# Chunked attention and a low-rank mixer: the last twelve tiles in three groups of four instead of four groups of three

## The chip, the cores and the metric

The kernel runs on one core of one Trainium2 chip. The metric is the device time of one execution in microseconds (us), the median of several runs. The engines are PE (matrix products; its weight loads are listed apart as PEld), DVE (vector work), ACT (activations), POOL (GpSimd) and SP (SyncE, which here only issues transfers).

## The reference

```python
# q, k, v: (8 batches, 8 heads, 576 positions, 64), fp32
q_c = q.reshape(B, H, nc, 64, D)            # 9 chunks of 64 positions; the same for k and v
scores = scale * np.matmul(q_c, k_c.transpose(0, 1, 2, 4, 3))
scores = scores - np.max(scores, axis=-1, keepdims=True)
attn = np.exp(scores)
attn = attn / (np.sum(attn, axis=-1, keepdims=True) + 1e-09)
x = np.matmul(attn, v_c)                    # heads side by side: x is (8, 576, 512)
u = x + (x.transpose(0, 2, 1) @ U @ V).transpose(0, 2, 1)     # U 576 x 32, V 32 x 576
out = u + np.maximum(u @ w_ch1, 0.0) @ w_ch2                  # 512 -> 2048 -> 512
```

## The kernel before

The 8 x 576 positions are 36 tiles of 128 positions, four pairs of batches with nine tiles each; tile T is number t = T mod 9 of pair T div 9, and names in the program end in pair and tile (`av0_3_1` is tile 28). All large products are made from fp32r values split into a high and a low part, three products for one (high x high, high x low, low x high).

A tile's attention takes these steps. q and k were laid out again in HBM by transfers (`halvings`), are loaded (`load`), and turned on DVE in 32 x 32 squares (`qT`, `kT`, L463). `scores` makes `sc` on PE: 32 small matmuls of 64 x 64. DVE takes the maxima (`mx`) and subtracts them (`ex`), ACT makes the exponentials, and SP's queue writes them to HBM and fetches them back re-laid (`es`), so that one more DVE transpose gives `eT`. `values` makes `av` on PE, 32 small matmuls again; DVE divides by the sums and leaves `x`. For the mixer, PE makes `y` (from `x` and U, `project_ops`) once a batch's tiles are there, and `u` (from `y` and V, L692); DVE adds `u` to `x` (L698); `x` then goes through HBM and a DVE transpose (`us`, `uT`), or for the first pair through four PE transposes (`ut`, L704), and is split by ACT (`uth`, L724) and DVE (`utl`, L729).

The channel product runs over groups of three tiles, 384 columns. For each of 16 blocks f of 128 hidden channels, `hidden` makes twelve matmuls (`h`, L757), `relu_high` on ACT (L766) and `relu_low` on DVE (L771) leave `hh` and `hl`, and one block later `project_out` (L784), called by `flush` tile by tile, adds three 512-column matmuls per tile into that tile's accumulator (`o`, one PSUM bank per tile, eight banks in all). After the last block `finish` (L796) adds the residual `x` and SP's queue writes the tile out.

Groups 0 and 1 are ordered by a planner that knows costs. From group 2 on, the work on later tiles is put between the flushes by lists of words, spread evenly over a group's slots: `n` load, `t` turn q and k, `s` scores, `q` turn the exponentials, `a` the last step (`av` and its division), `p` one step of `y`, `l`, `f`, `u` the three steps of the mixer, `h` a halving transfer. `scores` brings the previous tile's last step with it:

```python
        soft = behind[-1][0]
        done = behind.pop(0)[2] if len(behind) > 1 else []
        return [*done, *soft]
```

A scheduler then settles the order of instructions within each engine, near to where the program's order has them. Residuals `x` stay in SBUF (nine buffers) from their attention to their `finish`.

Of the kernel before, what the change touches and what calls it, by code (L numbers as in the profile page):

```python
# [22 lines left out]
def kernel(  # L23
# [17 lines left out]
    P = 128  # L41
# [44 lines left out]
    ident = const.tile([P, P], F32, name="ident")  # L86
    make_identity(nc, ident)
    warm = const.tile([P, 1], F32, name="warm")
    nc.scalar.activation(warm, ident[:, 0:1], AF.Exp)
# [52 lines left out]
    def begin_filling():  # L142
        spare["a"] = const.tile([P, 512], mybir.dt.bfloat16, name="fill")
        nc.vector.memset(spare["a"], 0.0)
        spare["ps"] = bank("ps_fill")
        fill(7)
# [232 lines left out]
    ut_of = {}  # L379
# [23 lines left out]
    def load_qk(pr, t):  # L403
# [63 lines left out]
    def attention_ops(pr, t, *after):  # L467
# [48 lines left out]
        def maximum(e):  # L516
            if e == 0:
                st["ex"] = slot(tag_e, F32, "ex_" + n, (P, HP, 2, C) if own else (P, 2, C // SQ, HP, SQ))
                st["mx"] = work.tile([P, 2, HP], F32, tag="mx", name="mx_" + n, bufs=2)
# [44 lines left out]
        def sums():  # L564
            sm = st["sm"] = work.tile([P, 2, HP], F32, tag="sm", name="sm_" + n, bufs=2)
# [66 lines left out]
    def project_ops(pr, e, xs):  # L632
        steps = []
        prev = None
        for i in range(5):
# [3 lines left out]
            def high(i=i, n=n, st=st):  # L639
                st["h"] = slot("uT", F32R, "xh_" + n)  # L640
                nc.scalar.copy(st["h"], x_of[pr, i + 4 * e])  # L641
# [28 lines left out]
            steps.append([h, lo, prev])  # L670
# [11 lines left out]
    def mix_ops(pr, t, x, ys, after=None, first=None):  # L682
        n = f"{pr}_{t}"
        st = {}
        g, j = divmod(t, GT)
# [19 lines left out]

        def put_u():
            st["kept"] = put(x_of[pr, t], "us_" + n, by_channel=True)

        def fetch_u():
            st["us"] = fetch(st["kept"], slot("us", F32, "us_" + n, (P, P // SQ, P)))  # L710

        def square_u():
            uT = st["t"] = slot("uT", F32, "uT_" + n)
# [4 lines left out]
        def high():  # L718
            if j == 0:
                ut_of[pr, g] = [  # L720
                    work.tile([P, NCC, GN], F32R, tag="ut" + z, name=f"ut{z}_{pr}_{g}", bufs=2) for z in "hl"
                ]
            ptv = st["t"].rearrange("p (c t) -> p c t", c=NCC)
            nc.scalar.copy(ut_of[pr, g][0][:, :, j * P : (j + 1) * P], ptv)  # L724

        def low():
            uh, ul = ut_of[pr, g]
            js = slice(j * P, (j + 1) * P)
            nc.vector.tensor_sub(ul[:, :, js], st["t"].rearrange("p (c t) -> p c t", c=NCC), uh[:, :, js])  # L729
# [4 lines left out]
        if (pr, t) == (0, 0):  # L734
            Op("PE", 0.01, end_filling, lr, free="bank")
        if pr > 0:
# [5 lines left out]
            return [[lr, ad, pu], [fe], [tr, hi, lo]]  # L742
# [6 lines left out]
    def hidden(pr, g, f):  # L749
        uh, ul = ut_of[pr, g]  # L750
        ps = bank(f"h_{pr}_{g}_{f}")
        w = w1[f]
        prods = [(0, uh), (0, ul), (1, uh)]
        n = 0
        for cc in range(NCC):
            for z, u in prods:
                o = nc.tensor.matmul(  # L757
                    ps[:, :GN], lhsT=w[:, z, cc], rhs=u[:, cc, :], start=(n == 0), stop=(n == 3 * NCC - 1)
                )
                n += 1  # L760
# [32 lines left out]
    def finish(pr, g, f, j, ps):  # L793
        t = g * GT + j
        x = x_of[pr, t]
        nc.vector.tensor_add(x, ps, x)  # L796
        if f == NF - 1:
            r0 = pr * 2 * S + t * P
            nc.sync.dma_start(out_f[r0 : r0 + P], x)

    def block_ops(pr, g, f, first, final, after, prev):
# [3 lines left out]
        def h():  # L805
            st["ps"] = hidden(pr, g, f)

        def rh():
            st["hh"] = relu_high(pr, g, f, st["ps"])

        def rl():
            st["hl"] = relu_low(pr, g, f, st["ps"], st["hh"])

        def out(j):
            st[j] = project_out(pr, g, f, (st["hh"], st["hl"]), first, final, j)
# [7 lines left out]
        for j in range(GT):  # L823
            d = Op("PE", 0.7, lambda j=j: out(j), c, d, take="bank" if first else "", free="h" if j == GT - 1 else "")
            if final:
                ends.append(
                    Op("DVE", 0.69, lambda j=j: finish(pr, g, f, j, st[j]), d, free="bank x" if last else "bank", lat=2.0)
# [13 lines left out]
    TAIL = 6  # L841
# [9 lines left out]
    for item in WORK:  # L851
# [13 lines left out]
        else:  # L865
            for t in range(GT * i, GT * i + GT):
# [14 lines left out]
    for g, f0, f1 in STRETCHES:  # L881
        for f in range(f0, f1):
            rank[0] = BASE
            prev = block_ops(0, g, f, f == 0, f == NF - 1, [*w_done[f], *mixed[g]], prev)
# [36 lines left out]
    tiles = [(pr, t) for pr in range(NPAIR) for t in range(NT)]  # L921
    pend = None

    def flush(j):
        if pend is not None:
            pr, g, f, hs = pend
            ps = project_out(pr, g, f, hs, f == 0, f == NF - 1, j)
            if f == NF - 1:
                finish(pr, g, f, j, ps)
# [3 lines left out]
    def attend(pr, t, what):  # L933
# [16 lines left out]
    LATER = {  # L950
# [95 lines left out]
```

## Time and profile before

| | us |
|---|---|
| median of 3 runs (lowest to highest) | 940.14 (939.91 to 940.99) |
| the profiled execution: its time | 939.42 |
| its span in the trace | 937.6 |
| granted clock of PE, mean | 0.996 |

The profile is that of one execution. Spans, starts and waits are microseconds of its span, which is 1.8 us shorter than the execution's time. PE's matmuls overlap, and their ends are modelled, so that a matmul's cost is read from the start of one to the start of the next. A granted clock of 1.00 is the upper of PE's two levels, 2.4 GHz.

### The profile page before, as it was taken

How to read it: one execution, taken by the hardware profiler on the slowest of the kernel's cores; microseconds unless marked ns; L12 is line 12 of the kernel's file. 1: busy time of each engine (PE TensorE's matmuls, PEld its weight loads, DVE VectorE, ACT ScalarE, POOL GpSimd, SP SyncE). 2: the span in 40 equal slices, each digit the busy share in tenths (PEclk: the TensorE clock that was granted, in tenths of full speed). 3: DMA queues.
4: the chain of work that ended last, by engine and by line, in shares of the span. 5: the costliest groups of instructions: out<-in, count | busy, mean ns of one | idle time of the engine just before them, and what ended most of it. 6: DMA issues, size and time to landing. Idle time of an engine off the chain costs nothing.

```text
span 937.6 us, 16153 instructions
## 1 busy us (share of the span) xinstructions
PE 916.5 (98%) x6639; PEld 806.1 (86%) x6642; DVE 488.7 (52%) x922; ACT 212.3 (23%) x379; POOL 30.1 (3%) x84
## 2 busy tenths in 40 slices
PE   7789999999999999999999999999999999999998
PEld 4569999878898888888898898988889889999997
DVE  6789999975545535553434534553433643321211
ACT  5434343322211212121211221111121211111110
POOL 5510000000000000000000000000000000000000
PEclk9999999999999999999999999999999999999999
DMA  9980688546646535563543733562231512310000
GB/s 214 222 260 1 140 168 185 138 129 146 143 98 150 127 57 130 124 127 81 129 92 79 153 70 79 150 140 68 78 91 35 148 45 46 79 23 1 35 1 34
DMA packets 271449, 98.79 MB, mean 105 GB/s; under 512 B 221296, under 2 KB 257136, under 8 KB 271376
## 3 DMA queue, kind: packets, MB, share of 16 engines
q1 hardware_dynamic: 269440, 94.81, 44.5%
q0 software_dynamic: 1328, 2.80, 1.4%
q8 instruction: 52, 0.85, 0.4%
q10 hardware_dynamic: 608, 0.15, 0.1%
q14 instruction: 21, 0.17, 0.1%
HBM read 73.84 MB, written 37.75 MB: 119 GB/s over the span
## 4 chain that ended last, share of the span: by engine, by line
PE 91%; DMA 3%; DVE 3%; issue 1%; ACT 1%; SPq 0%; POOL 0%; DVEq 0%; ACTq 0%
PE h L757 43%; PE o L784 41%; DMA qkv<-in_q_dram 2%; PE av L555 2%; PE sc L507 2%; PE u L692 1%; PE y L652 1%; PE y L653 1%; DMA vall<-vroom 1%; PE y L659 1%; PE ps_fill L151 0%; DVE eT L463 0%; PE ps_qT L477 0%; DMA us<-us_3d 0%; PE ps_kT L477 0%
## 5 line engine op out<-in xcount | busy, mean ns | idle before, releaser
L757 PE MATMUL h<-uth,w 128*128 128x384 f32 x1536 | 413.5, 337 | 1.6 <-DVE ex L528 1.6
L784 PE MATMUL o<-w,hh 128*128 128x512 f32 x1152 | 346.6, 393 | 0.0
L757 PEld LDWEIGHTS h<-uth,w 128*128 128x128 f32 x1536 | 279.8, 188 | 10.6 <-issue 1.4
L757 PE MATMUL h<-utl,w 128*128 128x384 f32 x768 | 258.1, 336 | 1.3 <-DVE utl L729 1.3
L784 PEld LDWEIGHTS o<-w,hh 128*128 128x128 f32 x1152 | 213.8, 188 | 36.7
L784 PE MATMUL o<-w,hl 128*128 128x512 f32 x576 | 214.2, 396 | 0.0
L771 DVE SCALAR_TENSOR_TENSOR hl<-h,hh 128x384 fp32r<-128x384 f32 x192 | 105.5, 549 | 203.3 <-ACT hh L766 202.8
L766 ACT ACTIVATE hh<-h 128x384 fp32r<-128x384 f32 x192 | 94.4, 491 | 458.7 <-PE h L757 458.5
L757 PEld LDWEIGHTS h<-utl,w 128*128 128x128 f32 x768 | 144.1, 188 | 7.9 <-DVE utl L729 1.6
L784 PEld LDWEIGHTS o<-w,hl 128*128 128x128 f32 x576 | 107.4, 188 | 22.9
L463 DVE STREAM_TRANSPOSE uT<-us 128x512 f32<-128x512 f32 x27 | 29.6, 1097 | 50.7 <-PE h L757 26.9
L463 DVE STREAM_TRANSPOSE eT<-es 128x512 f32<-128x512 f32 x27 | 29.1, 1079 | 41.0 <-DMA es<-es_6d 9.5
L463 DVE STREAM_TRANSPOSE qT<-qn 128x512 f32<-128x512 f32 x27 | 19.1, 709 | 46.4 <-PE h L757 44.7
L536 ACT ACTIVATE ex<-ex 128x512 f32<-128x512 f32 x36 | 22.8, 634 | 72.4 <-DVE ex L528 60.2
L641 ACT CAST xh<-x 128x512 fp32r<-128x512 f32 x30 | 18.5, 618 | 69.7 <-DVE x L574 44.7
L698 DVE TENSOR_TENSOR x<-u,x 128x512 f32<-128x512 f32 x36 | 24.2, 685 | 19.2 <-PE u L692 19.0
L521 DVE TENSOR_REDUCE mx<-sc 128x4 f32<-128x256 f32 x72 | 27.9, 413 | 5.4 <-PE sc L507 5.4
L724 ACT CAST uth<-uT 128x512 fp32r<-128x512 f32 x27 | 16.7, 620 | 53.6 <-DVE uT L463 53.6
L574 DVE TENSOR_TENSOR x<-av,sm 128x256 f32<-128x256 f32 x72 | 27.2, 419 | 1.4 <-DMA out_dram<-x 0.3
L414 POOL MEMSET vn<- 128x8 f32 x27 | 3.1, 114 | 689.1 <-PE av L555 506.3
L796 DVE TENSOR_TENSOR x<-o,x 128x512 f32<-128x512 f32 x36 | 23.1, 677 | 3.6 <-PE o L784 3.6
L645 DVE TENSOR_TENSOR xl<-x,xh 128x512 fp32r<-128x512 f32 x30 | 20.6, 686 | 7.6 <-ACT xh L641 6.8
(85 smaller groups left out, 531.7 us busy)
## 6 DMA issues: line engine op xcount, KB each, us to landing
wraw<-in_moe_w_ch_dram SPq DMA_DIRECT2D x32, 512.0 KB
out_dram<-x SPq DMA_DIRECT2D x36, 256.0 KB
halfq<-in_q_dram SPq DMA_DIRECT2D x24, 288.0 KB
halfk<-in_k_dram SPq DMA_DIRECT2D x24, 288.0 KB
qn<-halfq SPq DMA_DIRECT2D x27, 256.0 KB
kn<-halfk SPq DMA_DIRECT2D x27, 256.0 KB
vn<-in_v_dram SPq DMA_DIRECT2D x108, 64.0 KB
qkv<-in_v_dram POOLq DMA_DIRECT2D x36, 64.0 KB, 7.3
```

Of the source, the lines that this page charges most:

```text
L463: turned = nc.vector.transpose(dst, src)
L507: nc.tensor.matmul(ps[e][cs, hp * C : (hp + 1) * C], lhsT=st["qT_"][rows, hp, cs], rhs=st["kT_"][rows, hp, cs], start=True, stop=True,)
L521: nc.vector.reduce_max(mx, st["sc"][e], axis=AX.X)
L536: nc.scalar.activation(exf, exf, AF.Exp, scale=SCALE)
L574: nc.vector.tensor_mul(by_head[:, heads(pr, t, e), :], st["av"][e][:, :, 0:D], st["sm"][:, e].unsqueeze(2).broadcast_to([P, HP, D]),)
L645: nc.vector.tensor_sub(st["l"], x_of[pr, i + 4 * e], st["h"])
L698: nc.vector.tensor_add(x, st["u"], x)
L757: o = nc.tensor.matmul(ps[:, :GN], lhsT=w[:, z, cc], rhs=u[:, cc, :], start=(n == 0), stop=(n == 3 * NCC - 1))
L766: nc.scalar.activation(hh, ps[:, :GN], AF.Relu)
L771: nc.vector.scalar_tensor_tensor(hl, ps[:, :GN], 0.0, hh, op0=ALU.max, op1=ALU.subtract)
L784: nc.tensor.matmul(acc[g, j], lhsT=h[:, js], rhs=w2[f][:, z], start=(first and i == 0), stop=(final and i == 2),)
L796: nc.vector.tensor_add(x, ps, x)
```

## The change

Tiles 0 to 23 stay in eight groups of three. Tiles 24 to 35 become three groups of four: 24 to 27, then 30, 31, 28, 29, then 32 to 35; their `hidden` matmuls have 512 columns, with 48 blocks in place of 64. What goes with it:

- The words now carry the slot at which they are due, one list for each group from 2 on. `scores` no longer brings the previous tile's last step; that is the word `a`. The product of a `y` step is a word of its own (`y`).
- The split transposed input `ut` becomes one constant pair of buffers of six tiles, in which a group has its place (`PLACES`); `hh`, `hl`, the identity and the filler share one constant `hbuf`; the softmax sums live in a column of `vn`, and `mx` has one buffer.
- The residuals of tiles 21 to 35 are written to HBM (`put_rest`) and read back (word `r`) on GpSimd's queue. q, k and v of tiles 29 to 35 are loaded on that queue too.
- Tile 27 is transposed on PE (`TURNED`), not through HBM and DVE.
- Tiles 27, 30, 31, 34 and 35 (`LATE`) get their high and low split behind the last `hidden` of the group before; at the end of those groups the pending `project_out` is done at once.

```diff
+    WIDE = 24
+    KEPT = 21
+    GROUPS = [[T, T + 1, T + 2] for T in range(0, WIDE, 3)]
+    GROUPS += [[24, 25, 26, 27], [30, 31, 28, 29], [32, 33, 34, 35]]
+    PLACES = [0, 3, 0, 3, 0, 3, 0, 3, 0, 2, 0]
+    LATE = {7: [27], 8: [30, 31], 9: [34, 35]}
+    TURNED = (27,)
...
+    hbuf = const.tile([P, 4, 512], F32R, name="hbuf")
...
+    ident = hbuf[:, 3, 3 * P :].bitcast(F32)
...
+    ut = [const.tile([P, NCC, 6 * P], F32R, name="ut" + z) for z in "hl"]
...
-                nc.sync.dma_start(
+                queue = nc.sync if pr * NT + t < 29 else nc.gpsimd
+                queue.dma_start(
...
-                queue = nc.gpsimd if early(pr, t) else nc.sync
+                queue = nc.gpsimd if early(pr, t) or pr * NT + t >= 29 else nc.sync
...
-            steps.append([h, lo, prev])
+            steps.append([h, lo])
+            steps.append([prev])
...
+        def put_rest():
+            if T >= KEPT:
+                rest[pr, t] = dram.tile([P, DM], F32, name="rest_" + n)
+                nc.gpsimd.dma_start(rest[pr, t], x_of[pr, t])
+
...
+        if T in TURNED:
+            tr = Op("PE", 0.55, transposed, ad, take="bank")
+            hi = Op("ACT", 0.59, high, tr)
+            lo = Op("DVE", 0.69, low, hi, free="bank")
+            return [[lr, ad, put_rest], [], [tr], [hi, lo]]
...
-            return [[lr, ad, pu], [fe], [tr, hi, lo]]
+            return [[lr, ad, pu], [fe, put_rest], [tr], [hi, lo]]
...
-        soft = behind[-1][0]
-        done = behind.pop(0)[2] if len(behind) > 1 else []
-        return [*done, *soft]
+        return behind[-1][0]
...
-        1: "l6 t0 f6 s0 l7 n1 u6 f7 h t1 q0 s1 l8 n2 u7 f8 h t2 q1 s2 h n3 h u8 t3 . q2 s3 h n4 . .",
...
+        "h@0 t29@1 l24@2 q28@3 m30@3 a28@5 f24@6 s29@7 l25@8 u24@11 w24@11 f25@12 t30@13 l26@14 q29@15 m31@15 a29@17 u25@18 w25@18 f26@18 s30@18 u26@23 w26@23 t31@25 q30@27 p@27 m32@28 a30@29 s31@30 y@31 p@31 y@33 p@34 y@36 p@37 q31@38 y@39 a31@40 p@43 y@46 t32@49 l27@51 m33@51 s32@53 r21@54 u27@55 r22@56 r23@58",
...
+        elif kind == "r":
+            x_of[at] = work.tile([P, DM], F32, tag="x", name=f"rest_{T}", bufs=NX)
+            nc.gpsimd.dma_start(x_of[at], rest[at])
...
+    for g, words in enumerate(LISTS, 2):
...
+        late = [z for T in LATE.get(g, []) for z in (f"u{T}", f"w{T}") if z not in asked]
+        width = len(GROUPS[g])
...
+            for j in range(width + 1):
+                while words and int(words[0].split("@")[1]) <= slots:
+                    go(words.pop(0).split("@")[0])
                 slots += 1
...
+                if f == NF - 1 and j > 0 and late:
+                    go(late.pop(0))
+                flush(j)
+            pend = g, f, hs
+        assert not words and not late
+        if g in LATE:
+            for j in range(width):
+                flush(j)
+            pend = None
```

In the rows below a name ends in the numbers of pair and tile (`av0_3_1`: first half of the `av` of tile 28, number 1 of the last pair) or of group and tile, and in a buffer's number. On PE, around the `av` of tile 28 and the scores of tile 29, before:

```order
L784 MATMUL o_2_5_5980<-w_8_1457,hh_2_1_8_6269 128x512 x2
L555 MATMUL av0_3_1_6281<-vn_3_1_6014,eT_3_1_6273 64x65 x2
L555 MATMUL av1_3_1_6282<-vn_3_1_6014,eT_3_1_6273 64x65 x2
...
L555 MATMUL av1_3_1_6282<-vn_3_1_6014,eT_3_1_6273 64x65 x2
L507 MATMUL sc0_3_2_6306<-kT_3_2_6251,qT_3_2_6249 64x64 x2
L507 MATMUL sc1_3_2_6307<-kT_3_2_6251,qT_3_2_6249 64x64 x2
```

Before, the scores follow the `av` directly. After:

```order
L807 MATMUL o_7_0_5808<-w_0_248,hbuf_76 128x512 x3
L565 MATMUL av0_3_1_5812<-vn_3_1_5506,eT_3_1_5781 64x65 x2
L565 MATMUL av1_3_1_5813<-vn_3_1_5506,eT_3_1_5781 64x65 x2
...
L565 MATMUL av1_3_1_5813<-vn_3_1_5506,eT_3_1_5781 64x65 x2
L807 MATMUL o_7_1_5836<-w_0_248,hbuf_76 128x512 x3
L807 MATMUL o_7_2_5844<-w_0_248,hbuf_76 128x512 x3
L517 MATMUL sc0_3_2_5848<-kT_3_2_5761,qT_3_2_5759 64x64 x2
L517 MATMUL sc1_3_2_5849<-kT_3_2_5761,qT_3_2_5759 64x64 x2
```

Six `project_out` matmuls now stand between the two runs. On PE, around the `av` of tile 30 and the scores of tile 31, before:

```order
L784 MATMUL o_2_7_6679<-w_2_1072,hh_2_2_2_6700 128x512 x2
L784 MATMUL o_2_8_6683<-w_2_1072,hh_2_2_2_6700 128x512 x2
L555 MATMUL av0_3_3_6719<-vn_3_3_6364,eT_3_3_6714 64x65 x2
L555 MATMUL av1_3_3_6720<-vn_3_3_6364,eT_3_3_6714 64x65 x2
...
L555 MATMUL av1_3_3_6720<-vn_3_3_6364,eT_3_3_6714 64x65 x2
L507 MATMUL sc0_3_4_6744<-kT_3_4_6706,qT_3_4_6704 64x64 x2
```

This was one run of 64. After:

```order
L807 MATMUL o_7_2_5844<-w_6_1297,hbuf_76 128x512
L565 MATMUL av0_3_3_6140<-vn_3_3_5785,eT_3_3_6106 64x65
L807 MATMUL o_7_0_5808<-w_6_1297,hbuf_76 128x512
L565 MATMUL av0_3_3_6140<-vn_3_3_5785,eT_3_3_6106 64x65
L565 MATMUL av1_3_3_6141<-vn_3_3_5785,eT_3_3_6106 64x65 x2
...
L565 MATMUL av1_3_3_6141<-vn_3_3_5785,eT_3_3_6106 64x65 x2
L807 MATMUL o_7_1_5836<-w_6_1297,hbuf_76 128x512
L517 MATMUL sc0_3_4_6167<-kT_3_4_6098,qT_3_4_6096 64x64 x2
```

The `av` is now broken after its first matmul, and another `project_out` matmul stands between it and the scores. On DVE, around the `eT` of tile 30 (`eT_3_3`), before:

```order
L771 SCALAR_TENSOR_TENSOR hl_2_2_1_6667<-h_2_2_1_6652,hh_2_2_1_6665 128x384
L645 TENSOR_TENSOR xl_3_0_2_6675<-x_3_2_6477,xh_3_0_2_6673 128x512
L463 STREAM_TRANSPOSE qT_3_4_6704<-qn_3_4_6536 128x2x2x4x32
L463 STREAM_TRANSPOSE eT_3_3_6714<-es_3_3_6507 128x4x128
L771 SCALAR_TENSOR_TENSOR hl_2_2_2_6702<-h_2_2_2_6687,hh_2_2_2_6700 128x384
L463 STREAM_TRANSPOSE kT_3_4_6706<-kn_3_4_6537 128x2x2x4x32
```

and after, where `hbuf` written from `h` is what was `hl`:

```order
L531 TENSOR_REDUCE mx_3_3_6037<-sc0_3_3_6018 128x4
L531 TENSOR_REDUCE mx_3_3_6037<-sc1_3_3_6019 128x4
L538 TENSOR_TENSOR ex_3_3_6036<-sc0_3_3_6018,mx_3_3_6037 128x4x2x32
L538 TENSOR_TENSOR ex_3_3_6036<-sc1_3_3_6019,mx_3_3_6037 128x4x2x32
L473 STREAM_TRANSPOSE uT_2_8_6074<-us_2_8_6014 128x4x128
L795 SCALAR_TENSOR_TENSOR hbuf_76<-h_7_5_6050,hbuf_76 128x384
L745 TENSOR_TENSOR utl_86<-uT_2_8_6074,uth_85 128x4x128
L473 STREAM_TRANSPOSE qT_3_4_6096<-qn_3_4_5955 128x2x2x4x32
L473 STREAM_TRANSPOSE eT_3_3_6106<-es_3_3_6045 128x4x128
L795 SCALAR_TENSOR_TENSOR hbuf_76<-h_7_6_6078,hbuf_76 128x384
L473 STREAM_TRANSPOSE kT_3_4_6098<-kn_3_4_5956 128x2x2x4x32
```

The order `qT`, `eT`, `relu_low`, `kT` stays; ahead of it now stand the softmax pieces of the same tile (`mx`, `ex`), the `uT` transpose of tile 26 and its `low` step, with one `relu_low` among them.

## Rows read from the trace of the kernel before

**Rows 1.** The profile's first block: busy time of each engine, its share of the span, and instructions.
```profile
PE 916.5 (98%) x6639; PEld 806.1 (86%) x6642; DVE 488.7 (52%) x922; ACT 212.3 (23%) x379; POOL 30.1 (3%) x84
```

**Rows 2.** Busy time by stretch of the span; columns: the stretch in us, its length, busy us and instructions of PE, PEld, DVE, ACT and POOL, the clock granted to PE, the busy share of the DMA engines, GB/s.
```profile
600.00:700.00 100.00, 100.00 (x790) 89.21 (x789) 44.53 (x96) 18.20 (x35) 0.57 (x5) 1.00 0.40 95
...
800.00:900.00 100.00, 100.00 (x507) 90.79 (x506) 23.23 (x38) 13.70 (x27) 0.00 (x0) 1.00 0.12 32
```

**Rows 3.** The waits of PE from 215 us to 932 us: what it waited for, us in total, times, longest.
```profile
PE y L652 <- DVE x L574: 0.2, 1, 0.2
```

**Rows 4.** The chain that ended last, its final pieces: start, length, what.
```profile
898.59 2.08 PE h L757 x12
900.67 2.06 PE o L784 x9
...
923.47 2.08 PE h L757 x12
...
933.69 0.69 DVE x L796
```

**Rows 5.** Timeline of PE where an `av` run and an `sc` run stand together: start us, length us, what (the length is that from the first start to the modelled end of the last matmul, so that pieces overlap; what counts here are the starts).
```profile
664.25 1.31 PE L784 MATMUL o<-w,hh 128*128 128x512 f32 x5
665.49 0.70 PE L555 MATMUL av<-vn,eT 64*64 64x65 f32 x32
666.00 0.65 PE L507 MATMUL sc<-kT,qT 64*64 64x64 f32 x32
666.58 0.96 PE L784 MATMUL o<-w,hl 128*128 128x512 f32 x3
667.38 0.34 PE L757 MATMUL h<-uth,w 128*128 128x384 f32 x1
```

**Rows 6.** Timeline of PE where an `av` run stands alone, same columns.
```profile
550.50 0.40 PE L784 MATMUL o<-w,hh 128*128 128x512 f32 x1
550.82 0.70 PE L555 MATMUL av<-vn,eT 64*64 64x65 f32 x32
551.45 0.50 PE L784 MATMUL o<-w,hh 128*128 128x512 f32 x1
551.79 0.39 PE L784 MATMUL o<-w,hl 128*128 128x512 f32 x1
```

**Rows 7.** Timeline of PE where an `sc` run stands alone.
```profile
585.00 0.40 PE L784 MATMUL o<-w,hl 128*128 128x512 f32 x1
585.33 0.69 PE L507 MATMUL sc<-kT,qT 64*64 64x64 f32 x32
585.96 0.73 PE L784 MATMUL o<-w,hh 128*128 128x512 f32 x2
586.52 0.39 PE L784 MATMUL o<-w,hl 128*128 128x512 f32 x1
```

**Rows 8.** Timeline of PE where an `av` run is broken in two.
```profile
460.35 1.31 PE L784 MATMUL o<-w,hh 128*128 128x512 f32 x5
461.60 0.33 PE L555 MATMUL av<-vn,eT 64*64 64x65 f32 x2
461.85 0.49 PE L784 MATMUL o<-w,hl 128*128 128x512 f32 x1
...
463.36 0.50 PE L784 MATMUL o<-w,hl 128*128 128x512 f32 x1
463.69 0.39 PE L784 MATMUL o<-w,hh 128*128 128x512 f32 x1
```

**Rows 9.** Timeline of PE around one of the four-transpose turns of the first pair of batches.
```profile
197.84 0.60 PE L704 MATMUL ut<-ident,x 128*128 128x128 f32 x4
198.19 0.71 PE L784 MATMUL o<-w,hh 128*128 128x512 f32 x2
198.75 0.40 PE L784 MATMUL o<-w,hl 128*128 128x512 f32 x1
```

**Rows 10.** Timeline of DVE and of PE's weight loads around the scores of one tile; in brackets the idle time before a piece and what ended it.
```profile
725.63 1.04 DVE L463 STREAM_TRANSPOSE eT<-es 128x512 f32<-128x512 f32 x1
...
726.53 0.54 DVE L771 SCALAR_TENSOR_TENSOR hl<-h,hh 128x384 fp32r<-128x384 f32 x1
...
726.99 0.69 DVE L463 STREAM_TRANSPOSE kT<-kn 128x512 f32<-128x512 f32 x1
...
727.73 0.56 PEld L507 LDWEIGHTS sc<-kT,qT 64*64 64x64 f32 x32 [0.22 <-DVE kT L463]
```

**Rows 11.** Timeline of SyncE's queue and of DVE around the trip of one tile's softmax values through HBM, and one row of the list of what DVE stood idle for ahead of the `eT` transposes (us, times).
```profile
761.68 0.36 SPq L459 DMA_DIRECT2D es_8d<-ex  x1
...
764.02 0.33 SPq L400 DMA_DIRECT2D es<-es_8d  x1
...
764.92 0.56 DVE L771 SCALAR_TENSOR_TENSOR hl<-h,hh 128x384 fp32r<-128x384 f32 x1 [1.52 <-ACT hh L766]
...
766.83 1.09 DVE L463 STREAM_TRANSPOSE eT<-es 128x512 f32<-128x512 f32 x1 [1.35 <-DMA es<-es_8d]
...
  DMA es<-es_6d: 9.5, 3
```

**Rows 12.** The loads of the first pair of batches that GpSimd's queue issues: duration of one issue in ns as min/median/max, first and last start; and the time from issue to landing.
```profile
L438 POOL DMA_DIRECT2D qkv<-in_v_dram x36: 615/615/950, 2.6 to 50.9; - x36
...
DMA to landing us min/median/max: 4.3/7.3/8.3
```

More of the change, by code (lines that the diff above doesn't have):

```diff
@@ L378 @@
     y_of = {}
-    ut_of = {}
+    rest = {}
     halves = {}
@@ L640, in high @@
                 st["h"] = slot("uT", F32R, "xh_" + n)
-                nc.scalar.copy(st["h"], x_of[pr, i + 4 * e])
+                split = nc.scalar.copy(st["h"], x_of[pr, i + 4 * e])
+                if pr == NPAIR - 1:
+                    sync = mybir.DependencyInfo(mybir.DependencyClass.Sync, mybir.DependencyReason.DATA)
+                    tc.add_manual_dep(split.ins, hidden_last[-1].ins.name, sync, reason="not before this block")
             def low(i=i, n=n, st=st):
@@ L684, in mix_ops @@
         st = {}
-        g, j = divmod(t, GT)
+        T = pr * NT + t
+        g = next(i for i, z in enumerate(GROUPS) if T in z)
+        at = PLACES[g] + GROUPS[g].index(T)
+        j = 0 if T == min(GROUPS[g]) else 1
         def low_rank():
@@ L826, in block_ops @@
                 ends.append(
-                    Op("DVE", 0.69, lambda j=j: finish(pr, g, f, j, st[j]), d, free="bank x" if last else "bank", lat=2.0)
+                    Op("DVE", 0.69, lambda j=j: finish(g, f, j, st[j]), d, free="bank x" if last else "bank", lat=2.0)
                 )
@@ L840 @@
     GATES = (25, 27)
-    TAIL = 6
     HALVES_FROM = 8
@@ L865 @@
         else:
-            for t in range(GT * i, GT * i + GT):
+            for t in GROUPS[i]:
                 m = mix_ops(0, t, xs[t], ys, first=his.get(i))[1]
@@ L970, in go @@
             return
-        kind, i = word[0], int(word[1:])
-        if kind == "n":
-            key = pr + (g > 0) + i // NT, i % NT
-            if key[0] < NPAIR:
-                load(*key)
+        if kind in "py":
+            do(steps.pop(0))
             return
+        T = int(word[1:])
+        at = divmod(T, NT)
         if kind in "tsqa":
-            at = pr + 1 if g else pr
-            if at < NPAIR:
-                do(attend(at, i, {"t": "turn", "s": "scores", "q": "square", "a": "last"}[kind]))
-            return
@@ L998 @@
+    for g, words in enumerate(LISTS, 2):
+        words = words.split()
         slots = 0
+        asked = [z.split("@")[0] for z in words]
+        late = [z for T in LATE.get(g, []) for z in (f"u{T}", f"w{T}") if z not in asked]
+        width = len(GROUPS[g])
+        last = g == len(GROUPS) - 1
         for f in range(NF):
-            ps = hidden(pr, g, f)
-            hh = relu_high(pr, g, f, ps)
-            hs = hh, relu_low(pr, g, f, ps, hh)
-            for j in range(GT + 1):
-                slots += 1
-                while done < len(steps) and done * (NF * 4 - TAIL) < len(steps) * slots:
-                    go(pr, g, steps[done])
-                    done += 1
-                if j < GT:
-                    flush(j)
@@ L1010 @@
-            pend = (pr, g, f, hs)
-        assert done == len(steps)
+            ps = hidden(g, f)
+            hh = relu_high(g, f, ps)
+            hs = hh, relu_low(g, f, ps, hh)
+            for j in range(width + 1):
+                while words and int(words[0].split("@")[1]) <= slots:
+                    go(words.pop(0).split("@")[0])
+                slots += 1
+                if f == NF - 1 and j > 0 and late:
+                    go(late.pop(0))
+                flush(j)
+            pend = g, f, hs
@@ L1012 @@
+        assert not words and not late
[3 more added lines that the diff above has]
+            pend = None
     with tc.manual_schedule(engines=None):
-        for j in range(GT):
+        for j in range(len(GROUPS[-1])):
             flush(j)
-    assert not to_halve
+    assert not to_halve and not steps
 _INS = ["q", "k", "v", "moe_U", "moe_V", "moe_w_ch1", "moe_w_ch2"]
```

134 lines of the change are left out of this document (57 added, 77 removed), and 10 rows, old and new, of tables (LATER, LISTS).

## The prediction

> **What bounds the kernel now.** I read the busy table first: PE is busy 916.5 of 937.6 us, 98% of the span, and the next engine, DVE, 52% [rows 1]. A share over the whole span can hide stages, so the table by stretches came next: between 600 and 700 us PE is busy for all of the 100 us at a granted clock of 1.00, and the same between 800 and 900; DVE has 44.5 and 23.2 us of work there and the DMA engines 40% and 12% [rows 2]. The list of waits says the same from the other side: from 215 to 932 us PE waited for another engine once, for 0.2 us [rows 3]. So the time is that of the PE stream: a microsecond more or less of PE work is a microsecond of the end, and everything on DVE, ACT and the queues counts only where it makes PE stand. The chain that ended last gives the prices: the twelve 384-column matmuls of `hidden` take 2.08 us, the nine 512-column matmuls of `project_out` 2.06 us, and from 898.59 to 923.47 six blocks pass, (923.47 - 898.59) / 6 = 4.147 us each; after the last matmul there is one 0.69 us addition [rows 4].
>
> **The wide groups.** The last twelve tiles need 4 x 16 = 64 blocks of 12 + 9 matmuls; afterwards 3 x 16 = 48 blocks of 12 + 12, all of 512 columns. The number of columns that pass is the same (12 x 384 x 64 = 12 x 512 x 48), so only the cost per column can change. Before: 64 x 4.147 = 265.4 us. After, if a 512-column `hidden` matmul costs what a 512-column `project_out` matmul costs, 2.06 / 9 = 0.229 us (0.2294 with the digits that the six blocks give): 48 x 24 x 0.2294 = 264.3. That is -1.1 us. The other bound takes the rate of `hidden` itself, 173.5 ns for 384 columns, 231.3 for 512: 48 x 12 x (231.3 - 229.4) ns = 1.1 us back, so 0. I take -1.1, since the new matmul has the shape of `project_out`. A rule speaks here too: the Trainium skill, "TensorE: Matmul & The Clock Gate", on back-to-back issue, has a warm matmul cost its columns at 2.4 GHz plus about 2.5 ns. By the page 768 matmuls of 162.5 ns would become 576 of 215.8 ns, -0.5 us, and the sum below would be 0.6 higher; the rows are 7% above its figures at both sizes, so its offset is not used.
>
> **More separate runs of small matmuls.** The attention of a tile is two runs of 32 matmuls on 64 x 64 parts of the array, `av` and `sc`. Before, `scores` of a tile brought the previous tile's `av` with it, so that the two stand as one run. The new lists issue them by separate words, and the order of PE shows them apart, with `project_out` between. What that costs is read from starts. A pair: from 664.25 to 667.38 lie the run and eight `project_out` matmuls, 3.13 - 8 x 0.2294 = 1.29 us for the pair [rows 5]. `av` alone: 550.50 to 551.79 less two, 0.83 us [rows 6]. `sc` alone: 585.00 to 586.52 less three, 0.83 us [rows 7]. So a pair that is parted costs 0.83 + 0.83 - 1.29 = 0.37 us. A tile whose `av` is broken by one `project_out` matmul: 460.35 to 463.69 less seven, 1.73 us, 0.44 more than the whole pair [rows 8]. The rows show where it goes: the matmul ahead of a run lasts 550.82 - 550.50 = 0.32 us from its start to that of the run, not 0.229, and the one behind it 0.34 [rows 6]; the rest is the run's own beginning and end. The Trainium skill, "TensorEngine Tiling (Array Packing)", Key Properties, states that changing the tiling mode drains TensorE. It gives no figure; by it the price hangs on the number of entries and not on that of the matmuls, and a count of matmuls alone (the same before and after) would put this term at 0 and the sum at 940.
>
> Counted in the order of PE from the scores of tile 27 on, there are 11 runs before and 24 after: seven pairs are parted and six runs more come from `av` or `sc` broken in pieces. 7 x 0.37 + 6 x 0.44 = **+5.2 us**. The bounds: at least the lengthened neighbours, 0.09 + 0.11 = 0.20 us each [rows 6], 13 x 0.20 = 2.6; at most 0.44 for every one, 5.7.
>
> **Tile 27 turned on PE.** Four transposes come into the PE stream, and a trip through HBM with a DVE transpose goes. From 197.84 to 198.75 lie four transposes and two `project_out` matmuls: 0.91 - 0.46 = **+0.45 us** [rows 9].
>
> **Waits of PE on DVE.** PE's one listed wait comes with a y product; the weight load for the scores at 727.73 stood 0.22 us for `kT` as well, which stands on DVE behind `eT` and a `relu_low` [rows 10]. The same order (`qT`, `eT`, `relu_low`, `kT`) is there after, but groups 6 and 7 hold four to five attention tiles rather than three, and uT transposes with their `low` steps come close ahead. The trip of the softmax values takes 766.83 - 761.68 = 5.15 us from its first issue to the `eT` that waited for it, and another tile's `eT` waited 9.5 / 3 = 3.2 us for them three times [rows 11] without holding PE, since DVE had nothing due. In the new lists a tile's square (`q`) stands 8 to 11 slots behind its scores (`s29@7`, `q29@15`), a slot being a quarter of a 4.15 us block or a fifth of a wide one of 24 x 0.2294 = 5.5 us, so 1.0 to 1.1 us. The trip with some 3 us of softmax ahead of it (my estimate from the pieces around it) then just fits, with no slack to speak of. I take +0.3 us over before; the bounds are 0 and +3.
>
> **Costed at nothing.** The residuals of tiles 21 to 35 make 15 transfers out and 15 in of 256 KB. The DMA engines are busy 40% and later 12% of the time [rows 2], and a residual is asked for (`r` words) nine or more slots ahead of its addition, some 10 us, where loads on GpSimd's queue land in 4.3 to 8.3 us [rows 12]. Without that cover the one addition and its output wait, not PE, except at the tail, where the last `r` stands a block and more ahead. The loads of tiles 29 to 35 move from SyncE's queue to GpSimd's: an issue costs 615 ns there [rows 12], SyncE gets that time free, and GpSimd has nothing else. Wider `relu_high` and `relu_low` lie beside 5.5 us of PE per block. At the ends of groups 7, 8 and 9 the pending `project_out` is done at once behind the last `hidden`; the late uT split (ACT, DVE) and the last `relu` pair are covered by 24 of these matmuls, 2 x 2.75 us, and if they weren't, PE would stand for what is missing, three times. The tail stays: one 0.69 us addition behind the last matmul [rows 4]; each tile's three matmuls, 0.69 us, keep pace with it. The one conversion more at the start (128 columns, on DVE) is a fraction of a microsecond at most, once, and I give it nothing.
>
> **Sum.** -1.1 + 5.2 + 0.45 + 0.3 = +4.9 us on the profiled execution's 939.42, 944.3; the median of the runs is 0.72 above that execution, so **945.0 us**. With all bounds: low -1.1 + 2.6 + 0.45 + 0 = +2.0, 942.1; high 0 + 5.7 + 0.45 + 3 = +9.2, 949.3.
>
> **Rivals.** The bound of what a measurement of this kernel can tell is 0.2%, 1.9 us: slower means above 942.0, faster below 938.3.
> - DVE comes late in groups 6 to 8. PE's order is fixed, so where an `eT` comes later than foreseen, the `av` or the `kT` with its scores holds PE for that time. Against it: PE stood only 0.2 us in the whole stretch before. For it: the waits of 1.35 and 3.2 us in rows 11 show how much one trip varies. If that difference, 1.9 us, lands on two tiles, 945.0 + 3.7 = 948.7. It decides from the point where DVE has less than about 2 us free between scores and square. Chance 0.13.
> - The runs are cheaper than sized. The new fragments lie between the same matmuls, and part of the lengthening seen around a run may come once for several pieces that stand close together. At 0.1 us each, 1.3 in place of 5.2: 941.1, no change that can be told. Rows 8 speak against it. Chance 0.09.
> - Not slower, by the wide `hidden`: if a 512-column matmul with moving columns from one constant buffer has less fixed cost than rows 4 show, 576 of them each give it back. To come within 0.2% each must be at 229.4 - 3.0 / 0.576 = 224.2 ns; at 220 ns the end is 945.0 - 5.4 = 939.6; to be faster, below 217.8. Against it: the rate per column is within 1% at 384 and 512 columns, so there is little fixed cost to save. Chance 0.05.
>
> The forecast keeps 0.73. Slower holds it, the DVE rival, and little else: 0.86. Within 0.2%: most of the two cheaper cases, 0.10. Faster: 0.04, the far end of the wide rival and what I have not seen. The range 941.5 to 949.0 takes in both sums of bounds but for 0.3 us at the top, and leaves out about 2 in 10 with the cheap cases below and the far end of the DVE case above.
>
> **What would show it.** Right: in the wide groups starts of `hidden` matmuls 229 ns apart and blocks of 5.50 us; single runs of `av` and `sc` at 0.83 us net; four transposes near 0.45; PE still at 98% or more of the span, its waits under 1 us. Wrong: `hidden` at 224 ns or less; runs whose neighbours start on time; PE waits on `eT`, `kT`, a bank or `ut` at the head of groups 8 to 10; a first half that isn't the same as before to 0.3 us.

## The result, and the profile after

The changed kernel takes 948.07 us (median of 6 runs, 947.45 to 948.88), the kernel before 940.57 us in the runs beside it: a ratio of 1.0079, 95% interval 1.0066 to 1.0092. That is slower by 7.5 us. The forecast was 945.0 us and slower by 4.9 us. The profiled execution took 948.83 us, near the top of its runs, with a span of 947.1 us against 937.6 before.

The table by stretches shows where PE is no longer busy all the time. With the columns of [rows 2], first one stretch of the kernel before and then the changed kernel:

```profile
500.00:600.00 100.00, 99.76 (x728) 88.59 (x728) 48.97 (x97) 18.78 (x36) 0.45 (x4) 1.00 0.50 113
```

```profile
500.00:600.00 100.00, 95.93 (x810) 83.31 (x810) 53.13 (x114) 17.89 (x34) 9.29 (x20) 0.98 0.64 147
600.00:700.00 100.00, 99.67 (x748) 83.48 (x747) 50.29 (x102) 19.02 (x35) 27.15 (x48) 1.00 0.43 120
...
800.00:900.00 100.00, 100.00 (x443) 82.81 (x442) 18.86 (x27) 12.33 (x21) 0.00 (x0) 1.00 0.03 12
```

Between 500 and 600 us 4.1 us of PE are gone; before, 0.2 were. From 800 us on PE has no gap. The waits of PE from 206 us to the end, in the columns of [rows 3]:

```profile
PE av L565 <- issue: 4.6, 3, 2.7
PE h L779 <- DVE x L584: 0.6, 1, 0.6
PE o L807 <- DVE hbuf L795: 0.3, 1, 0.3
```

One wait of 0.2 us has become five of 5.5 us together, and most of it is ahead of `av`, put down to nothing that the list can name ("issue"). The end of the chain, as in [rows 4]:

```profile
880.50 2.72 PE h L779 x12
883.22 2.72 PE o L807 x12
885.93 2.72 PE h L779 x12
...
934.89 2.72 PE h L779 x12
937.62 5.45 PE o L807 x24
...
943.09 0.69 DVE rest L819
```

The wide groups are faster than forecast: both kinds of matmul take 2.72 us for twelve, and a block takes 885.93 - 880.50 = 5.43 us, over a longer stretch 5.440, so 226.6 ns for each matmul and not 229.4. 48 x 5.44 = 261.1 us stand against 265.4 before: -4.3 us, where the prediction had -1.1.

The longest wait is at 591 us, ahead of the `av` of tile 28 (in this trace `es_1` of the last pair). The timeline of SyncE's queue, DVE and PE there:

```profile
585.01 0.36 SPq L469 DMA_DIRECT2D es_1d<-ex  x1
...
585.46 0.77 SPq L398 DMA_DIRECT2D halfk<-in_k_dram  x1
...
587.41 2.08 SPq L409 DMA_DIRECT2D es<-es_1d  x1
...
592.60 1.08 DVE L473 STREAM_TRANSPOSE eT<-es 128x512 f32<-128x512 f32 x1 [4.94 <-DMA es<-es_1d]
...
593.75 0.59 PEld L565 LDWEIGHTS av<-vn,eT 64*64 64x64 f32 x32 [3.11 <-issue]
593.78 0.70 PE L565 MATMUL av<-vn,eT 64*64 64x65 f32 x32 [2.70 <-issue]
```

The softmax values are written at 585.01. A halving transfer (`halfk`, 288 KB, for a later tile) comes next in the queue, and the fetch of the softmax values behind it takes 2.08 us to issue, where it took 0.33 in [rows 11]. `eT` starts 5.2 us after the fetch and not 2.8; DVE stands for 4.94 us, and PE for 2.70. What follows is seen in the stretches around it (columns as in [rows 2]) and in PE's timeline:

```profile
586.00:590.00 4.00, 4.00 (x22) 3.61 (x21) 1.66 (x3) 0.49 (x1) 0.59 (x1) 1.00 0.84 170
590.00:594.00 4.00, 1.30 (x19) 0.85 (x21) 1.40 (x2) 0.49 (x1) 0.00 (x0) 1.00 0.80 164
594.00:598.00 4.00, 4.00 (x71) 2.83 (x62) 3.54 (x10) 0.00 (x0) 0.82 (x2) 0.61 0.64 231
598.00:602.00 4.00, 4.00 (x24) 3.69 (x21) 2.93 (x6) 1.51 (x3) 3.19 (x5) 0.97 0.66 207
```

```profile
594.41 2.57 PE L807 MATMUL o<-w,hbuf 128*128 128x512 f32 x6
596.91 1.13 PE L517 MATMUL sc<-kT,qT 64*64 64x64 f32 x32
```

PE was busy for 1.30 of the 4 us in which it stood; in the next 4 us the granted clock is 0.61. Of the six `project_out` matmuls that begin there the first two starts lie 0.33 us apart and the next three 427 ns, which is 512 columns at the lower level of 1.2 GHz. Worked out from the starts, what PE did from 594.4 to 598.4 cost 1.5 us more than the same instructions cost at the upper level. The Trainium skill, "TensorE: Matmul & The Clock Gate", on what is actually happening, says that the clock is throttled by default and that activity releases it; the rows agree.

### The profile page after: what moved, and what is told of

It is laid out like the page before. It is cut to its first block, busy times and chain, and to the rows that moved or that the text cites. A ratio compares the mean times of both kernels' runs of the same rounds, so it can differ in the third digit from the quotient of the medians.

```text
span 947.1 us, 15846 instructions
## 1 busy us (share of the span) xinstructions
PE 921.8 (97%) x6451; PEld 785.4 (83%) x6454; DVE 485.1 (51%) x906; ACT 209.4 (22%) x363; POOL 74.1 (8%) x156
## 4 chain that ended last, share of the span: by engine, by line
PE 89%; DMA 5%; DVE 3%; issue 1%; ACT 1%; POOL 0%; SPq 0%; DVEq 0%; ACTq 0%; POOLq 0%
PE h L779 41%; PE o L807 40%; PE av L565 2%; PE sc L517 2%; DMA qkv<-in_v_dram 2%; DMA qkv<-in_q_dram 1%; PE u L709 1%; PE y L666 1%; PE y L665 1%; DMA out_dram<-x 1%; PE y L672 1%; DVE x L584 0%; DMA es<-es_2d 0%; PE ps_qT L487 0%; DMA us_8d<-x 0%
## 5 line engine op out<-in xcount | busy, mean ns | idle before, releaser
L807 PE MATMUL o<-w,hbuf 128*128 128x512 f32 x1728 | 433.8, 394 | 0.4 <-DVE hbuf L795 0.3
L779 PE MATMUL h<-uth,w 128*128 128x384 f32 (+1 forms) x1408 | 405.3, 352 | 2.3 <-DVE ex L538 1.6
L807 PEld LDWEIGHTS o<-w,hbuf 128*128 128x128 f32 x1728 | 321.4, 188 | 65.0 <-DVE hbuf L795 1.2
L779 PEld LDWEIGHTS h<-uth,w 128*128 128x128 f32 x1408 | 259.1, 188 | 23.7 <-PE sc L517 1.9
L779 PE MATMUL h<-utl,w 128*128 128x384 f32 (+1 forms) x704 | 246.7, 350 | 1.3 <-DVE utl L745 1.3
L795 DVE SCALAR_TENSOR_TENSOR hbuf<-h,hbuf 128x384 fp32r<-128x384 f32 (+1 forms) x176 | 103.0, 585 | 211.1 <-ACT hbuf L790 210.3
L790 ACT ACTIVATE hbuf<-h 128x384 fp32r<-128x384 f32 (+1 forms) x176 | 91.6, 520 | 467.9 <-PE h L779 467.6
L473 DVE STREAM_TRANSPOSE uT<-us 128x512 f32<-128x512 f32 x26 | 28.5, 1096 | 55.0 <-PE h L779 16.4
L565 PE MATMUL av<-vn,eT 64*64 64x65 f32 x864 | 21.2, 225 | 4.7 <-issue 4.6
L448 POOL DMA_DIRECT2D qkv<-in_v_dram x36 | 22.5, 632 | 18.5 <-PE ps_qT L487 10.8
L745 DVE TENSOR_TENSOR utl<-uT,uth 128x512 fp32r<-128x512 f32 x26 | 17.9, 687 | 7.5 <-ACT uth L741 7.5
```

The lines of the kernel that those rows point to most:

```text
L448: d = queue.dma_start(vn[e * C : (e + 1) * C, c, :, 0:D], v[b, heads(pr, t, e), s0 : s0 + C, :].rearrange("h s d -> s h d"),)
L473: turned = nc.vector.transpose(dst, src)
L565: nc.tensor.matmul(ps[e][cs, hp * D1 : (hp + 1) * D1], lhsT=st["eT_"][rows, hp, cs], rhs=vn[rows, c, hp, :], start=True, stop=True,)
L779: o = nc.tensor.matmul(ps[:, :n], lhsT=w[:, z, cc], rhs=ut[u][:, cc, cols], start=(i == 0), stop=(i == 3 * NCC - 1))
L790: nc.scalar.activation(hh, ps[:, 0 : len(GROUPS[g]) * P], AF.Relu)
L795: nc.vector.scalar_tensor_tensor(hl, ps[:, 0 : len(GROUPS[g]) * P], 0.0, hh, op0=ALU.max, op1=ALU.subtract)
```

## The experiments

Four kernels were run beside one another on one chip: the moved halving transfers, the collision made in the kernel before, the rejoined steps and the 512 columns. On a second chip ran the changed kernel, the moved halvings again and the two trials with the residual writes; on a third the rejoining without writes and the two trials with the loads; on a fourth the writes in the kernel before. Runs of one kernel spread by 2.5 to 9.2 us, and those of the kernel before by 3.5 to 6.5 us on one chip, so that medians are compared within one chip, with the interval of the ratio to the kernel before. A profile shows a single execution, which lay up to 2.3 us off the median of its runs.

**Halving transfers moved.** The order of SyncE's queue has a halving transfer between the write and the fetch of the softmax values for exactly five tiles: 13, 16, 25, 26 and 28. Each was moved behind the fetch, in the lists of groups 2, 3, 6 and 7:

```diff
-        "... s14@34 h@35 m15@37 ...
+        "... s14@34 m15@37 ... h@44 ...
...
-        "... t17@21 h@22 q16@24 ... m18@29 h@30 ...
+        "... t17@21 q16@24 ... h@28 m18@29 h@30 ...
...
-        "... t26@21 h@22 q25@24 ... h@34 q26@35 a26@36 p@38 y@38 h@39 ...
+        "... t26@21 q25@24 ... h@28 ... q26@35 a26@36 p@38 y@38 h@39 h@39 ...
...
-        "h@0 t29@1 l24@2 q28@3 m30@3 a28@5 f24@6 ...
+        "t29@1 l24@2 q28@3 m30@3 a28@5 h@5 f24@6 ...
```

> The changed kernel with five of its 32 halving transfers moved in SyncE's queue, so that none stands between the write of a tile's softmax values and their fetch; nothing else differs. Theory A (a fetch issued right behind a halving transfer is held): the five fetches whose issue took 1.9 to 2.1 us take 0.33 us like the other 22, their eT starts about 2.8 us after the fetch and not 4.5 to 5.2, PE's stalls ahead of av at tiles 13, 25, 26 and 28 go (1.6 + 1.25 + 0.17 + 2.77 us, and some 1.5 us of lowered clock behind the last), 7.3 us in all: 940.5 to 941.5. Theory B (DVE is late because groups 6 and 7 hold more attention work): eT waits as before, PE's stalls stay within 1.5 us: 946.5 or more.

Measured: 946.21 us, before 941.16, ratio 1.0050 (1.0026 to 1.0074). On the second chip it stood beside the changed kernel:

> The changed kernel itself, so that it stands beside the kernel before and the two that follow on one chip. Expected: 947 to 949.5, 0.8% above before, with five softmax fetches whose issue takes about 2 us.

> The kernel with the five halving transfers moved, on the chip of the changed kernel. By the first profile of it the stalls ahead of av fell from 5.8 us to 0.5 and one of 1.9 us came in their place behind the uT of tile 26, so 4 us below the changed kernel (944 to 945.5); if the gain was the chip's, no difference.

Measured there: the changed kernel 947.22 us (1.0055, 1.0034 to 1.0077), the moved one 945.97 (1.0035, 1.0019 to 1.0051). The fetches, in the list of transfers of `es` (issue in ns as min/median/max, three tiles a row), of the changed kernel in the profile of the result and then of the moved one on the second chip:

```profile
L409 SPq DMA_DIRECT2D es<-es_1d x3: 337/338/2076, 196.1 to 587.4; - x3
...
L409 SPq DMA_DIRECT2D es<-es_7d x3: 332/2037/2132, 312.1 to 705.2; - x3
```

```profile
L409 SPq DMA_DIRECT2D es<-es_1d x3: 333/337/338, 196.1 to 584.5; - x3
...
L409 SPq DMA_DIRECT2D es<-es_7d x3: 332/338/338, 311.3 to 699.7; - x3
```

All fetches are back at 0.33 us. PE's 5.5 us of waits became 2.9 us in the first profile of the moved kernel and 1.5 us in the second:

```profile
PE o L807 <- DVE hbuf L795: 2.0, 2, 1.7
PE av L565 <- issue: 0.9, 2, 0.7
```

```profile
PE av L565 <- issue: 0.8, 1, 0.8
PE o L807 <- DVE hbuf L795: 0.7, 1, 0.7
```

So theory A names a real cost, but its 7.3 us were too many: from profile to profile 4 us less (948.83 to 944.74, on two chips) or 3 us (946.62 to 943.65, on one), and 1.25 us between the medians of one chip, whose intervals overlap. What came in its place is seen in the first profile, around the `uT` of tile 26:

```profile
604.87 2.18 SPq L464 DMA_DIRECT2D us_8d<-x  x4
...
605.25 0.58 POOL L726 DMA_DIRECT2D rest<-x  x1
...
611.53 0.33 SPq L409 DMA_DIRECT2D us<-us_8d  x1
...
615.32 1.08 DVE L473 STREAM_TRANSPOSE uT<-us 128x512 f32<-128x512 f32 x1 [4.18 <-DMA us<-us_8d]
...
616.25 0.53 DVE L795 SCALAR_TENSOR_TENSOR hbuf<-h,hbuf 128x384 fp32r<-128x384 f32 x1
```

The four writes of `us` begin at 604.87, the write of the same tile's residual goes out on GpSimd's queue at 605.25, the fetch can be issued only at 611.53, and DVE stands 4.18 us for it with a `relu_low` behind, which PE waits for.

**The same collision made in the kernel before.** Two `h` words of one list were moved, so that for tiles 16 and 25 a halving transfer stands between write and fetch:

```diff
-        0: "t6 q5 s6 l3 n7 h f3 t7 q6 s7 u3 n8 h p0 t8 h q7 s8 p1 n9 h p2 . ...
+        0: "t6 q5 s6 l3 n7 h f3 t7 q6 s7 u3 n8 h p0 h t8 q7 s8 h p1 n9 p2 . ...
```

> The kernel before with the order of three words changed in one list, so that for tiles 16 and 25 a halving transfer stands between the write of the softmax values and their fetch. Theory A: these two fetches take about 2.0 us to issue, their eT comes 4.5 to 5.2 us after the fetch (2.7 to 2.9 now), PE stalls ahead of their av for 1 to 2 us each: 942.5 to 945. Theory B: no difference above 0.2%, 939.5 to 941.5.

Measured: 942.77 us, before 941.16, ratio 1.0015 (1.0003 to 1.0027). The two fetches take 1.1 us to issue, and their `eT` comes 3.75 us after the fetch:

```profile
L400 SPq DMA_DIRECT2D es<-es_7d x3: 337/1086/1150, 315.1 to 755.1; - x3
```

PE waits here:

```profile
PE h L757 <- DVE hl L771: 1.2, 1, 1.2
PE av L555 <- issue: 1.1, 2, 0.6
PE y L652 <- DVE x L574: 0.3, 1, 0.3
```

The collision is made again, but weaker (1.1 us to issue, where it was about 2), and the 1.6 us are not all its own: of the two tiles only 16 makes PE stand longer ahead of its `av`, by 0.5 us, and the wait of 1.2 us lies behind the `uT` of tile 21 and the `eT` of tile 24, which no halving transfer was put before; why these trips were late here is not settled. It supports the mechanism and not the size that theory A gave it.

**The last steps rejoined.** The words `a27` to `a30` were moved to the slot of the next tile's scores (`a28@5` to `a28@7`, and so on).

> The kernel of e1 with the last steps of tiles 27 to 30 moved to the slot of the next tile's scores, so that in the order of PE there are 20 runs of small matmuls from tile 27 on and not 25. By the price of the prediction, 0.37 us for a parted pair and 0.44 for a fragment: 4 x 0.37 + 0.44 = 1.9 us faster than e1. If runs cost 0.1 us each: 0.5 us faster. If the parting was what kept PE from waiting for banks or for DVE: slower than e1, with waits of sc on DVE in the trace.

Measured: 947.35 us (1.0064, 1.0048 to 1.0079), not below its base of 946.21. The runs did become cheaper: a joined pair costs 1.29 us by the starts, where two parted runs cost 0.83 us each, and all runs together cost 1.3 us less than in a profile of the base, not the 1.9 forecast. It is not seen in the time. PE's waits are 3.1 us, 2.9 in the base's profile from that chip, and now none is ahead of `av`.

**512 columns in one narrow group.**

```diff
-        n = len(GROUPS[g]) * P
+        n = 512 if g == 6 else len(GROUPS[g]) * P
```

> The kernel of e1, whose group 6 (three tiles) runs its hidden matmuls over 512 columns; the 128 columns more are not used. The question is why a project_out matmul costs 226.6 ns in the wide groups and about 230 in the narrow ones. If the 384-column matmuls around it are the cause: in group 6 project_out falls to 226.6 ns and hidden takes 226.6, the block 12 x 226.6 + 9 x 226.6 = 4.76 us. If it is something else of the late stage (less side work, fewer transfers): project_out stays near 230 ns in group 6. The 16 blocks cost 12 x 53 ns x 16 = 10.2 us more in either case, less 0.5 us in the first.

Measured: 957.65 us in one run. In group 6 seven `project_out` matmuls go from 565.51 to 567.10, 227 ns each:

```profile
565.51 1.75 PE L807 MATMUL o<-w,hbuf 128*128 128x512 f32 x7
567.10 0.40 PE L665 MATMUL y<-xh,ust 128*128 128x512 f32 x1
```

Between neighbouring `project_out` matmuls of the group the median from start to start is 227 ns (124 pairs), against 231 in the kernel it was made from (126 pairs). Nothing else was changed, the `relu` steps keep their width, and in the last stage of the kernel before, where side work and transfers are few, `project_out` is no cheaper (229.4, [rows 4]). So the 384-column matmuls around them are what made `project_out` dearer. Why they do is not shown.

**No residual writes.** The kernel with moved halvings, without the 15 writes. The 15 reads stay but fetch as many bytes of `q`, so that what is added at the end for tiles 21 to 35 is not their residual.

```diff
-                rest[pr, t] = dram.tile([P, DM], F32, name="rest_" + n)
-                nc.gpsimd.dma_start(rest[pr, t], x_of[pr, t])
+                rest[pr, t] = None
+            return
...
-            nc.gpsimd.dma_start(x_of[at], rest[at])
+            nc.gpsimd.dma_start(x_of[at], q[0, 0:2].rearrange("h s d -> (h s d)")[0 : P * DM].rearrange("(p c) -> p c", c=DM))
```

> The kernel of e1 without the 15 writes of residuals to HBM; the 15 reads stay, but take other data of the same size, so the residual of tiles 21 to 35 is wrong data. Theory C (the writes, issued beside the us transfers of the same tile, delay these trips): the time from the last us write to the fetch, up to 4.5 and 5.5 us for tiles 22 and 26, falls to the 1.5 to 3.2 us of the kernel before, the uT of tile 26 no longer holds relu_low, and PE's 1.9 us stall goes: 1.5 to 2.5 us below e1. Theory D (the residuals are free, as the prediction costed them): no difference from e1 above 0.5 us, and the trip of tile 26 stays above 4 us.

Measured: 942.17 us, 3.8 us below its base on the same chip; ratio to before 1.0003 (0.9987 to 1.0019). The list of PE's waits after 206 us is empty, and the stage is full:

```profile
500.00:600.00 100.00, 99.88 (x836) 87.37 (x835) 56.20 (x118) 19.64 (x37) 8.46 (x18) 1.00 0.67 147
600.00:700.00 100.00, 99.96 (x746) 83.29 (x746) 51.20 (x103) 20.02 (x36) 23.32 (x41) 1.00 0.40 109
```

Theory C holds for the time, with more than the 1.5 to 2.5 us it forecast. The waits seen explain only part of it: the profiled execution of the base has 1.5 us of them and stands 1.4 us above this one (943.65 and 942.26). From the end of a tile's last `us` write to the issue of its fetch, the 14 trips of tiles 21 to 35 take 2.73 us on average and not 3.35; at tile 22 it is 4.1 and not 5.4. One detail fell: the trip of tile 26 still has 4.2 us there, and PE no longer waits behind it.

**Residual writes later.** The write got a dependency on the `hidden` block at which `uT` is turned.

> The kernel of e1 with every residual write held until the hidden block at which the tile's uT is turned (tile 27, which has no such trip, as it was). Theory C: the trips are free of the writes as in the kernel without them, 1 to 2 us below e1, if the writes don't then hold the loads behind them on GpSimd's queue. Theory D: as e1.

Measured: 948.33 us (1.0059, 1.0035 to 1.0082), no better than its base: two waits of about 2 us, one on `relu_low` behind `uT`, one on the division of the attention on DVE. The cost moved.

**Rejoined, without residual writes.** The two edits together.

> The kernel without residual writes (its reads take other data of the same size, so the residual of tiles 21 to 35 is wrong data), and with the last steps of tiles 27 to 30 rejoined to the next tile's scores: 20 runs of small matmuls where there were 25. With PE's waits out of the way the price of the runs should show in PE's own stream: 4 x 0.37 + 0.44 = 1.9 us less than the kernel without residual writes, so 1.0 to 1.5 us below the kernel before. If the parted runs bought freedom from waits, waits of sc or relu on DVE appear and the time is that of before or above.

Measured: 946.83 us, before 942.05, ratio 1.0051 (1.0028 to 1.0075). PE, which waited for nothing without the rejoining, waits again:

```profile
PE o L807 <- DVE hbuf L795: 2.2, 1, 2.2
PE o L807 <- DVE x L715: 1.2, 1, 1.2
PE h L779 <- DVE hbuf L795: 1.2, 1, 1.2
PE av L565 <- issue: 0.4, 1, 0.4
PE sc L517 <- DVE x L819: 0.3, 1, 0.3
```

A joined pair puts `av` and the next scores back to back, so that the next tile's softmax comes together with this tile's division on DVE. That is my reading of the order; what the runs show is that 5.3 us of waits stand against runs that are 1.1 us cheaper by the starts (1.9 forecast). The parted runs bought freedom from waits in these groups.

**Loads back on SyncE's queue**, alone and with the later writes:

```diff
-                queue = nc.sync if pr * NT + t < 29 else nc.gpsimd
+                queue = nc.sync
-                queue = nc.gpsimd if early(pr, t) or pr * NT + t >= 29 else nc.sync
+                queue = nc.gpsimd if early(pr, t) else nc.sync
```

> The kernel of e1 (halving transfers moved, residuals written as in the changed kernel) with the loads of tiles 29 to 35 back on SyncE's queue. The prediction costed the queue at nothing. If that holds: as e1, 4.3 us above before, within 1 us. If GpSimd's loads delayed the trips: faster by 1 us or more. If SyncE's queue, in which the us writes and fetches stand, is now held by loads that wait for their buffers: slower by 1 us or more, with longer us trips.

> As the run before, and every residual write held until the hidden block at which the tile's uT is turned, with nothing but these writes and the residual reads on GpSimd's queue in that stage. If the held writes lost in the earlier trial because the loads stood behind them: now 1 to 3 us below e1, 942 to 945. If a write delays whichever trip comes next: no better than e1.

Measured: 947.26 us (1.0048, 1.0030 to 1.0065) and 946.14 us (1.0046, 1.0032 to 1.0061), before 942.05. Neither is told apart from the kernel with moved halvings (1.0035, 1.0019 to 1.0051). The queue of the loads is worth nothing that can be measured, as costed. In the trace of the second kernel the `us` trips are shorter than without any residual writes (2.47 us from last write to fetch on average, against 2.73), but tile 31's softmax values take 4.8 us from write to fetch and not 2.6, and PE waits 3.1 us. So short `us` trips alone do not bring the time back; what makes PE wait in these two kernels is not settled.

**Residual writes alone, in the kernel before.**

```diff
-            return [[lr, ad, pu], [fe], [tr, hi, lo]]
+            def put_rest():
+                if pr * NT + t >= 21:
+                    nc.gpsimd.dma_start(dram.tile([P, DM], F32, name="rest_" + n), x_of[pr, t])
+            return [[lr, ad, pu], [fe, put_rest], [tr, hi, lo]]
```

> The kernel before, with the 15 residual writes of tiles 21 to 35 added on GpSimd's queue at the place where the changed kernel has them; nothing reads them. If a residual write costs time by itself: 3 us or more above before, as between the kernels with and without them. If it costs only where a trip through HBM has no slack left (groups 6 and 7 of the changed kernel): the us trips are longer here too, by 0.5 us or more, but PE hardly waits: within 1 us of before.

Measured: 945.00 us, before 940.60, ratio 1.0047 (1.0033 to 1.0060): 4.4 us for 15 writes that nobody reads. The first of the two outcomes came. PE's waits, which were 0.2 us:

```profile
PE h L760 <- DVE hl L774: 1.0, 2, 0.7
PE h L760 <- ACT uth L724: 0.6, 2, 0.4
PE y L652 <- DVE x L574: 0.5, 2, 0.2
PE av L555 <- issue: 0.4, 1, 0.4
```

and what DVE stood idle for ahead of the `uT` transposes from 500 us on (us, times), in this kernel and then in the kernel before:

```profile
  DMA us<-us_4d: 7.7, 2
  DMA us<-us_0d: 4.4, 1
```

```profile
  DMA us<-us_4d: 5.6, 2
  DMA us<-us_0d: 3.1, 1
```

The trips of `us` are longer at some tiles: from last write to fetch by 0.8 to 1.0 us at tiles 22, 23, 27, 31 and 32, and by 0.4 us on average over the 15, since some are shorter. Ahead of all these `uT` DVE stands 16.4 us for a fetch and not 12.4, and the `relu_low` or the split behind it reaches PE late. The waits listed make 2.5 us of the 4.4; this profiled execution (943.27 us) was the fastest of its five runs.

## Why the prediction was right, and where it was not

The sign held, and the time lies in the range, but that is in part luck: two errors cancel in part. With the wide groups at the -1.1 us of the sum, the same waits would have led to about 951.3 us, above the range. And what the sum had priced makes no difference that can be told, +0.5 us (-1.2 to +1.8) in the kernel without residual writes and with the halvings moved: that the changed kernel is slower at all comes from what the sum put at nothing or did not list.

- **Wide groups: mis-sized.** -4.3 us and not -1.1. The price was taken from `project_out` in a stream with 384-column matmuls (229.4 ns), and such a stream is itself slower; among 512-column matmuls alone it is 226.6. The rival "cheaper wide `hidden`" had the mechanism, but only for `hidden`: `project_out` got cheaper too.
- **Parted runs and the four transposes: held.** In the kernel without residual writes, where PE waits for nothing, the small matmuls and transposes with the lengthened starts around them cost about 6 us more than in the kernel before from 206 us on, against 5.2 + 0.45 forecast. With -4.3 this gives +1.7; that kernel measures +0.5 us (-1.2 to +1.8), and +2.8 between profiled executions.
- **Residuals at nothing: the step that failed.** The cover that I named was right for the reads: the kernel that keeps them and leaves out the writes has no wait of PE. But I asked only whether the residual itself comes in time. What was late was other traffic. The writes cost 3.8 us by taking them out and 4.4 us by adding them to the kernel before, and in both trials some of the `us` trips beside them are longer. The Trainium skill, "DMA: Bandwidth & Descriptors", on issuing engines not being separate queues, says that transfers of all issuing engines run on the same 16 engines and interleave; the longer trips agree, and the mean share of 40% in [rows 2] did not show it.
- **Halving transfers: not in the list at all.** The new lists place five of them between a write and its fetch. The order of SyncE's queue, which I read for loads, showed it. By the traces this was 3 to 4 us of the profiled execution, with 1.5 us of lowered clock; between medians it is 1.3 us and not clearly told from nothing. Tile 13's collision came in the first half, which the prediction wanted unchanged to 0.3 us: from the first `hidden` matmul of group 2 to that of group 3 it is 74.0 us and not 72.4.
- **Waits +0.3: failed.** What is left of +7.5 us after -4.3 and +6 is 5.8 us; the profiled execution, 0.8 us above the median, shows 5.5 us of waits and 1.5 us of lowered clock. The rival in which DVE comes late happened, at its "two tiles or more", but its cause was the transfers and not the denser attention work alone: without the writes DVE has 56 us of work between 500 and 600 us, more than the 53 of the changed kernel, and PE waits for nothing. That freedom hangs on the order: with the steps rejoined PE waits 5.3 us without any residual write.
- **Loads on GpSimd's queue, transitions and tail: held.** No wait stands at the heads of groups 8 to 10, and the tail is one addition of 0.69 us.

What stays open: by which way a write delays a trip, and where the part of its cost goes that no wait in a trace shows. No version here is faster than the kernel before.

## What to carry to other kernels

Where a chain of work goes out to HBM and back within a few microseconds, every transfer that the change adds or moves must be asked what it delays, and not only whether it arrives in time; a mean transfer share well below one is no cover. Read the order of the queue between each write and its fetch. And a price per instruction belongs to the stream that it was read in.

## What the runs showed of the hardware

- A fetch that stands behind a 288 KB transfer of 128-byte pieces in the same queue took 1.9 to 2.1 us to issue and not 0.33, and the `eT` that needs it started 1.8 to 2.1 us later after the fetch than with the transfer moved. In the kernel before, the same order gave 1.1 us and about 1 us.
- After PE had stood for 2.70 us the granted clock of the next 4 us was 0.61: the stall cost 1.5 us more, half as much again.
- 15 writes of 256 KB cost 4.4 us where nothing read them, with the DMA engines busy 53% of the time between 500 and 600 us and 41% between 600 and 700.
- A 512-column matmul costs 226.6 ns among its like and 230 to 231 ns in a stream with 384-column ones, which themselves cost 173.5.
